# Top-k attention and SwiGLU: scaling by the softmax sum moved behind the product with V, and a pipeline of two turns instead of four

## The chip, the cores and the metric

The kernel runs on one core of a Trainium2 chip. The metric is the device time of one execution in microseconds (us), given as the median over runs. In the profile, PE is the tensor engine (PEld its weight loads), DVE the vector engine, ACT the scalar engine, POOL the GpSimd engine, and SP the engine that issues most DMAs. Every engine works through its own queue strictly in order.

## What is computed

Attention with 8 batches, 8 heads, 576 positions and 64 dimensions per head keeps, for each query, the 32 largest scores; its output, seen as 4608 tokens of 512 numbers, goes through a SwiGLU block with 1536 hidden units. All is float32.

```python
scores = scale * np.matmul(q, k.transpose(0, 1, 3, 2))
kth = np.partition(scores, -top_k, axis=-1)[..., -top_k:-top_k + 1]
scores = np.where(scores >= kth, scores, -1000000000.0)
scores = scores - np.max(scores, axis=-1, keepdims=True)
attn = np.exp(scores)
attn = attn / (np.sum(attn, axis=-1, keepdims=True) + 1e-09)
x = np.matmul(attn, v)              # (B,H,S,D) -> (B*S, H*D)
g = x @ w_gate
out = (g / (1 + np.exp(-g)) * (x @ w_val)) @ w_out
```

## The kernel before

Attention is cut into 160 units: batch, a tile of 128 queries (`qt` 0 to 3) or the last 64 queries (`qt` 4), and a pair of heads. A unit of `qt` 0 to 3 holds two heads as 1152 columns on 128 partitions and is called a two-head unit here. In a unit of `qt` 4 the 64 queries of both heads stack to 128 partitions and 576 columns; the code calls it one head. A batch has 16 two-head and 4 one-head units.

The main loop (from line 729) makes one turn per unit. In turn n, DVE does the top-k of unit n (`select`): four rounds of MAX8 with three rounds of MATCH_REPLACE between, and a last pass (line 339) that writes a penalty mask into `e`. The other steps belong to units before or after n and stand in the same turn, so that each engine's order is written out by hand; at the end of the program the order of PE, DVE, ACT and POOL is pinned. SP's order is left to the scheduler.

In turn n before the change:

- `penalize(n-1)`: POOL computes the bias (line 349) and adds scores and mask (line 351).
- `turn(n-3)`: PE transposes the weights of unit n-3 (line 387), nine 128x128 blocks in a two-head unit; ACT copies them to `et` (line 388).
- `values(n-4)`: PE multiplies by V (lines 407 and 416); ACT copies the result into `xT` (line 431), the FFN's input.
- `scores(n+1)`: PE computes the next unit's scores (lines 308, 294); ACT copies them into `sc` (lines 313, 299).
- `weigh(n-1)`: ACT takes exponentials with their sums (line 360) and adds eps to the sums (line 365).
- `normalize(n-2)`: DVE takes reciprocals (line 372, after the fourth of the seven steps of its top-k), and ACT scales `e` by them (line 375).

Between these steps PE gets pieces of the FFN (`pieces`, `piece`, `feed`). A piece is four matmuls of 256 columns. A block of 256 tokens can start when all four head pairs of its queries are in `xT`. It has 24 product steps of four matmuls of 256 columns (line 471), whose results ACT and POOL combine into `h` (lines 496 to 504), and then seven quarters of six matmuls each (line 557). The quarters are a Strassen-like form of the output product, seven products of half-size blocks instead of eight, and need sums of `h` that POOL makes (lines 564, 572, 577, 605) and sums of results (line 543). The first block uses a plain output product. How many pieces a turn gets is set by `share`: 6.4 less the cost of the attention steps of that turn, in units of a piece. The ACT and POOL parts of a piece are put in lists and emitted at the next `flush`.

In the first 14 turns the weights are brought into a rounded form beside all that (`rounded`, lines 105 to 123: DMA, three ACT operations, one on DVE, two on POOL).

PSUM holds eight banks: five are shared by scores, transposes and products with V, and three by the FFN.

Of the kernel before, what the change touches and what calls it, by code (L numbers as in the profile page):

```python
# [8 lines left out]
AF = mybir.ActivationFunctionType  # L9
ALU = mybir.AluOpType  # L10
FP32 = mybir.dt.float32
# [4 lines left out]
P = 128  # L16
# [3 lines left out]
EPS = 1.0e-9  # L20
# [5 lines left out]
def kernel(  # L26
# [37 lines left out]
    nc = tc.nc  # L64
    B, H, S, D = q.shape
    DM, DFF = w_gate.shape
    J = S // P
    JP = J * P
    R = S - JP
# [9 lines left out]
    consts = ctx.enter_context(tc.tile_pool(name="consts", bufs=1))  # L79
    ld = ctx.enter_context(tc.tile_pool(name="ld", bufs=2))  # L80
    slabs = ctx.enter_context(tc.tile_pool(name="slabs", bufs=4))
    work = ctx.enter_context(tc.tile_pool(name="work", bufs=2))
# [2 lines left out]
    ffn = ctx.enter_context(tc.tile_pool(name="ffn", bufs=2))  # L85
    ps_t = ctx.enter_context(tc.tile_pool(name="ps_t", bufs=5, space=PSUM))
    ps_f = ctx.enter_context(tc.tile_pool(name="ps_f", bufs=3, space=PSUM))

    ident = consts.tile([P, P], FP32, name="ident")
    make_identity(nc, ident[:])  # L90
# [2 lines left out]
    for i in range(NV):  # L93
        vt = consts.tile([P, P], FP32, name=f"vlast{i}")
        nc.vector.memset(vt[:], 0.0)
        vlast.append(vt)
    eps = consts.tile([P, 1], FP32, name="eps")
    nc.vector.memset(eps[:], EPS)
    wg = consts.tile([P, KC, DFF], FP32, name="wg")
    wv = consts.tile([P, KC, DFF], FP32, name="wv")  # L100
    wo = consts.tile([P, MC, DM], FP32, name="wo")
# [170 lines left out]
    state = {}  # L272
# [5 lines left out]
    def scores(n):  # L278
        b, qt, hp = units[n]
        slab = preps[b * NHP + hp]  # L280
        sc = work.tile([P, 2 * S], FP32, tag="sc", name="sc", bufs=2)
        halves = [slice(0, D), slice(D, P)]
        half = S // 2

        def bank():
            return ps_t.tile([P, 512], FP32, tag="t", name="s")


        if qt == J:
            banks = [bank() for _ in range(2)]  # L290
            for i, ps in enumerate(banks):
                for d in halves:
                    k0 = R + i * half
                    nc.tensor.matmul(  # L294
                        ps[d, 0:half], slab[d, S + R : S + 2 * R], slab[d, k0 : k0 + half]
                    )
            yield
            for i, ps in enumerate(banks):
                nc.scalar.copy(sc[:, i * half : (i + 1) * half], ps[:, 0:half])  # L299
        else:  # L300
            q0 = S + 2 * R + qt * P
            banks = []
            for i in range(2):
                for hh, d in enumerate(halves):
                    ps = bank()
                    banks.append((i + 2 * hh, ps))
                    k0 = (1 - hh) * R + i * half
                    nc.tensor.matmul(  # L308
                        ps[:, 0:half], slab[d, q0 : q0 + P], slab[d, k0 : k0 + half]
                    )  # L310
            yield
            for i, ps in banks:
                nc.scalar.copy(sc[:, i * half : (i + 1) * half], ps[:, 0:half])  # L313
        state[n] = dict(sc=sc)

    def select(n):

        nh = n_heads(units[n][1])
        sc = state[n]["sc"]
        m = small.tile([P, 2, TOP_K], FP32, tag="m", name="m", bufs=2)  # L320
        heads = [slice(t * S, (t + 1) * S) for t in range(nh)]
        rest = work.tile([P, 2 * S], FP32, tag="rest", name="rest", bufs=1)
        e = work.tile([P, 2 * S], FP32, tag="e", name="e", bufs=4)
        state[n] |= dict(m=m, e=e, heads=heads)
        cur = sc
        rounds = TOP_K // 8
        for r in range(rounds):
            for t, hs in enumerate(heads):
                nc.vector.max(m[:, t, 8 * r : 8 * r + 8], cur[:, hs])  # L329
                yield  # L330
            if r < rounds - 1:
                for t, hs in enumerate(heads):
                    nc.vector.match_replace(  # L333
                        rest[:, hs], m[:, t, 8 * r : 8 * r + 8], cur[:, hs], LOWEST
                    )
                    yield
                cur = rest
        for t, hs in enumerate(heads):
            nc.vector.tensor_scalar(  # L339
                e[:, hs], sc[:, hs], m[:, t, TOP_K - 1 : TOP_K], FAR, ALU.is_lt, ALU.mult  # L340
            )
# [12 lines left out]
    def weigh(n):  # L354

        st = state[n]
        e, heads, bias = st["e"], st["heads"], st.pop("bias")
        tot = small.tile([P, 2], FP32, tag="tot", name="tot")
        for t, hs in enumerate(heads):
            nc.scalar.activation(  # L360
                e[:, hs], e[:, hs], AF.Exp, bias=bias[:, t : t + 1], scale=scale,
                accum_out=tot[:, t : t + 1],
            )
        nh = len(heads)
        nc.scalar.activation(tot[:, 0:nh], tot[:, 0:nh], AF.Identity, bias=eps[:])
        st["tot"] = tot

    def normalize(n):
        st = state[n]
        tot, e, heads = st.pop("tot"), st["e"], st.pop("heads")  # L370
        nh = len(heads)
        nc.vector.reciprocal(tot[:, 0:nh], tot[:, 0:nh])  # L372
        yield
        for t, hs in enumerate(heads):
            nc.scalar.mul(e[:, hs], e[:, hs], tot[:, t : t + 1])  # L375

    def turn(n):

# [19 lines left out]
    def values(n):  # L398

        b, qt, hp = units[n]  # L400
        vt, v_last, vl = vs[b * NHP + hp]
        et = state.pop(n)["et"]
        last = qt == J
        ql = R if last else P
        av = ps_t.tile([P, P], FP32, tag="t", name="av")
        if not last:
            nc.tensor.matmul(av[:], vl[:], et[:, J, :], start=True, stop=False)  # L407
        for c in range(J + 1 if last else J):
            kl = R if c == J else P
            for hh in range(2):  # L410
                moving = (
                    et[0:kl, c, hh * R : (hh + 1) * R]
                    if last
                    else et[:, c + hh * (J + 1), :]
                )
                nc.tensor.matmul(  # L416
                    av[hh * R : (hh + 1) * R, 0:ql],
                    v_last[:, hh, :] if c == J else vt[:, hh, c, :],
                    moving,
                    start=last and c == 0,  # L420
                    stop=c == (J if last else J - 1),
                )
        c0 = b * S + qt * P
        at = c0
        while at < c0 + ql:
            kb = at // BLK
            n_c = min((kb + 1) * BLK, c0 + ql) - at
            if kb not in xT:
                xT[kb] = ffn.tile([P, NHP, BLK], FP32, tag="xT", name="xT", bufs=3)
                done[kb] = 0  # L430
            nc.scalar.copy(
                xT[kb][:, hp, at - kb * BLK : at - kb * BLK + n_c],
                av[:, at - c0 : at - c0 + n_c],
            )
            done[kb] += n_c
            at += n_c
# [270 lines left out]
    def run(steps):  # L707
        for _ in steps:
            pass
# [13 lines left out]
    run(fetch(1))  # L723
    credit = [0.0]
    no = iter(())
    over = {}
    TURN, VALUES = 3, 4
    due = [2.0]
    for n in range(NU + VALUES):
        nh = n_heads(units[n][1]) if n < NU else 1  # L730
        topk = select(n) if n < NU else no
        over[n - 1] = normalize(n - 1) if 0 <= n - 1 < NU else no
        nxt = scores(n + 1) if n + 1 < NU else no
        ahead = fetch(n + 2) if n + 2 < NU else no
        norm = over.pop(n - 2, no)

        def dve(k, beside=True):

            for _ in range(k * nh):
                next(topk, None)  # L740
                due[0] += 5 / 6 if beside else 0
                if due[0] >= 1:
                    due[0] -= 1
                    rounding(1)

        if n >= NU - NHP:
            credit[0] = 8.0
        else:
            credit[0] = min(credit[0] + share(n), share(n) + 1)
        flush(on_act)  # L750
        if 0 <= n - 1 < NU:
            penalize(n - 1)
        flush(on_pool)
        if 0 <= n - TURN < NU:
            run(turn(n - TURN))
        if n >= VALUES:
            finish_unit(n - VALUES)
        next(nxt, None)

        early[0]()  # L760
        if 0 <= n - 1 < NU:
            weigh(n - 1)
        run(nxt)


        dve(2, beside=False)
        if 2 <= n + 2 < NHP:
            load(n + 2)
        if n < NHP:
            load_v(n)  # L770
        pieces(2)
        flush(on_act)
        dve(1)
        dve(1)
        next(norm, None)
        run(norm)

        flush(on_pool)
        next(ahead, None)
        pieces(1)  # L780
        next(ahead, None)
        dve(1)
        pieces(1)
        dve(2, beside=False)
        run(topk)
        pieces(6)
# [50 lines left out]
```

## Time and profile before

| | |
|---|---|
| median of 3 runs | 1821.17 us (1820.94 to 1823.55) |
| span of the profiled execution | 1817.8 us; the runs' median lies 3.4 us above it |
| instructions | 30526 |
| PE, DVE, ACT, POOL busy | 1708.7, 1610.7, 1218.7, 1036.4 us |
| DMA moved | 59.65 MB, mean 33 GB/s |

The profiled execution's own time is not recorded apart from its span, so that the two are compared through the median. Busy time is the union of an engine's instructions. Lines of the timeline give the start in us from the span's start, the duration, engine, source line, operation, what is written and read, and a count; idle time before the instruction and what ended it stand in brackets. An fp32 matmul appears in the profile as two records.

### The profile page before, as it was taken

The page shows a single profiled execution, that of the slowest core. Times are in us where ns is not written, and L with a number is a line of the kernel's source. Part 1 is how long each engine was busy: PE and PEld are TensorE (multiplying, and loading weights), DVE is VectorE, ACT ScalarE, POOL GpSimd, SP SyncE. Part 2 cuts the span into 40 slices and gives each one's busy share as a digit, 9 for nine tenths or more (in the row PEclk, how much of TensorE's full clock was granted, in tenths as well). Part 3 has the DMA queues.
Part 4 walks back from the last instruction along what each step waited for, and adds up shares of the span by engine and source line. Part 5 has one row for each costly group of instructions (what it writes and reads, how often), then busy time and mean ns, then how long its engine had stood idle before and what let it go on. Part 6 is the DMA issues. An engine that isn't in the chain of part 4 may idle for free.

```text
span 1817.8 us, 30526 instructions
## 1 busy us (share of the span) xinstructions
PE 1708.7 (94%) x10756; PEld 1409.2 (78%) x10756; DVE 1610.7 (89%) x3372; ACT 1218.7 (67%) x2977; POOL 1036.4 (57%) x930
## 2 busy tenths in 40 slices
PE   4458999899999899999999999999999999999999
PEld 2346778687788788887888878887888878888887
DVE  7999999999999799997999989998999989998400
ACT  6778666676667676666767676767676766675532
POOL 5788756455565645554455636564556554646354
PEclk6669999899999999999999999999999999999999
DMA  7432030002100030000300021000300011000000
GB/s 191 125 108 90 14 85 7 12 1 50 45 1 13 2 82 12 13 1 22 73 12 2 13 56 39 1 12 3 74 19 13 1 36 33 1 13 12 1 12 12
DMA packets 109305, 59.65 MB, mean 33 GB/s; under 512 B 88544, under 2 KB 96992, under 8 KB 109152
## 3 DMA queue, kind: packets, MB, share of 16 engines
q1 hardware_dynamic: 108016, 57.37, 12.1%
q8 instruction: 85, 1.39, 0.3%
q14 instruction: 68, 0.56, 0.1%
q10 hardware_dynamic: 1136, 0.33, 0.1%
HBM read 48.23 MB, written 9.44 MB: 32 GB/s over the span
## 4 chain that ended last, share of the span: by engine, by line
PE 86%; DVE 8%; ACT 2%; POOL 2%; issue 2%; DMA 0%; SPq 0%; ACTq 0%; POOLq 0%
PE f L471 41%; PE x_ps L557 9%; PE av L416 8%; PE etps L387 7%; PE s L308 7%; PE y_ps L557 7%; DVE m L329 3%; DVE rest L333 3%; PE s L294 2%; PE av L407 1%; PE o_ps L517 1%; PE kqps L263 1%; DVE size L121 1%; DVE e L339 0%; POOL p L543 0%
## 5 line engine op out<-in xcount | busy, mean ns | idle before, releaser
L329 DVE MAX8 m<-rest 128x8 f32<-128x576 f32 x864 | 612.7, 744 | 2.2
L351 POOL TENSOR_TENSOR e<-e,sc 128x1152 f32<-128x1152 f32 (+1 forms) x160 | 383.1, 2394 | 83.7 <-DVE e L339 76.3
L333 DVE MATCH_REPLACE8 rest<-m,rest 128x576 f32<-128x576 f32 x576 | 423.1, 740 | 0.0
L471 PE MATMUL f<-xT,wg 128*128 128x256 f32 x1728 | 401.6, 382 | 0.0
L471 PE MATMUL f<-xT,wv 128*128 128x256 f32 x1728 | 399.1, 382 | 0.0
L471 PEld LDWEIGHTS f<-xT,wg 128*128 128x128 f32 x1728 | 323.1, 190 | 62.6 <-issue 21.3
L471 PEld LDWEIGHTS f<-xT,wv 128*128 128x128 f32 x1728 | 324.5, 190 | 58.7 <-issue 16.6
L499 POOL TENSOR_TENSOR h<-h,half_g 128x512 f32<-128x512 f32 x108 | 138.2, 1280 | 292.7 <-ACT h L498 292.2
L329 DVE MAX8 m<-sc 128x8 f32<-128x576 f32 x288 | 205.0, 747 | 104.0 <-ACT sc L299 57.8
L388 ACT COPY et<-etps 128x512 f32<-128x512 f32 (+1 forms) x448 | 184.1, 483 | 131.0 <-PE etps L387 130.2
L360 ACT ACTIVATE e<-e,bias 128x576 f32<-128x576 f32 x288 | 222.1, 777 | 57.5 <-POOL e L351 57.2
L387 PE MATMUL etps<-ident,e 128*128 128x128 f32 (+1 forms) x1312 | 184.5, 286 | 79.3 <-POOL size L122 18.2
L504 POOL TENSOR_TENSOR h<-h,val 128x512 f32<-128x512 f32 x108 | 139.6, 1293 | 186.3 <-ACT val L503 186.1
L387 PEld LDWEIGHTS etps<-ident,e 128*128 128x128 f32 (+1 forms) x1312 | 159.6, 147 | 106.0 <-POOL size L122 20.7
L375 ACT ACTIVATE e<-e,tot 128x576 f32<-128x576 f32 x288 | 212.0, 790 | 0.9 <-DVE tot L372 0.9
L333 DVE MATCH_REPLACE8 rest<-m,sc 128x576 f32<-128x576 f32 x288 | 211.5, 740 | 0.0
L308 PE MATMUL s<-kqT 64*128 64x288 f32 x1024 | 178.8, 449 | 14.1 <-ACT kqT L268 8.3
L339 DVE TENSOR_SCALAR e<-sc,m 128x576 f32<-128x576 f32 x288 | 177.2, 651 | 3.4
L416 PE MATMUL av<-et,v 128*64 128x128 f32 (+1 forms) x2560 | 170.3, 278 | 0.0
L313 ACT COPY sc<-s 128x288 f32<-128x288 f32 x512 | 164.0, 402 | 2.9 <-PE s L308 2.9
L496 ACT ACTIVATE h<-f 128x512 f32<-128x512 f32 x108 | 65.2, 604 | 133.3 <-PE f L471 133.3
L416 PEld LDWEIGHTS av<-et,v 128*64 128x64 f32 x2560 | 134.1, 143 | 22.8 <-issue 6.8
(73 smaller groups left out, 2029.1 us busy)
## 6 DMA issues: line engine op xcount, KB each, us to landing
v<-in_v_dram SPq DMA_DIRECT2D x32, 256.0 KB, 2.9
kq_in<-in_k_dram SPq DMA_DIRECT2D x63, 128.0 KB, 2.8
kq_in<-in_q_dram SPq DMA_DIRECT2D x63, 128.0 KB, 3.0
w<-in_moe_w_gate_dram SPq DMA_DIRECT2D x12, 512.0 KB, 3.7
w<-in_moe_w_val_dram SPq DMA_DIRECT2D x12, 512.0 KB, 3.8
w<-in_moe_w_out_dram SPq DMA_DIRECT2D x12, 512.0 KB, 3.5
out_dram<-o SPq DMA_DIRECT2D x38, 128.0 KB, 2.4
out_dram<-o SPq DMA_DIRECT2D x16, 256.0 KB, 2.4
```

Source lines behind the costliest of these rows:

```text
L308: nc.tensor.matmul(ps[:, 0:half], slab[d, q0 : q0 + P], slab[d, k0 : k0 + half])
L329: nc.vector.max(m[:, t, 8 * r : 8 * r + 8], cur[:, hs])
L333: nc.vector.match_replace(rest[:, hs], m[:, t, 8 * r : 8 * r + 8], cur[:, hs], LOWEST)
L339: nc.vector.tensor_scalar(e[:, hs], sc[:, hs], m[:, t, TOP_K - 1 : TOP_K], FAR, ALU.is_lt, ALU.mult)
L351: nc.gpsimd.tensor_tensor(e[:, every], e[:, every], sc[:, every], ALU.add)
L360: nc.scalar.activation(e[:, hs], e[:, hs], AF.Exp, bias=bias[:, t : t + 1], scale=scale, accum_out=tot[:, t : t + 1],)
L375: nc.scalar.mul(e[:, hs], e[:, hs], tot[:, t : t + 1])
L387: nc.tensor.transpose(ps[0:kl, c * P : (c + 1) * P], e[:, k0 : k0 + kl], ident[:])
L388: nc.scalar.copy(et[0:kl, c0 : c0 + cn, :], ps[0:kl, 0 : cn * P].rearrange("p (c j) -> p c j", c=cn),)
L416: nc.tensor.matmul(av[hh * R : (hh + 1) * R, 0:ql], v_last[:, hh, :] if c == J else vt[:, hh, c, :], moving, start=last and c == 0, stop=c ...
L471: nc.tensor.matmul(ps[:, i, :], w[:, kc, m * P : (m + 1) * P], x[:, kc, :], start=(kc == 0), stop=(kc == KC - 1),)
L557: nc.tensor.matmul(ps, lhsT, T[i][m], start=m == 0, stop=m == MQ - 1)
```

## The change

The scaling by the reciprocal of the softmax sum is taken off the weights and put behind the product with V. `normalize` goes. The new `invert(n)` adds eps and takes the reciprocal on DVE, writes the reciprocals of a unit to a small DRAM tile and reads them back broadcast over partitions into `inv`, since the product with V has queries along its columns. `values` now copies its result to `avs`, and the new `scale_up(n)` multiplies `avs` by `inv` into `xT` on POOL.

The distance between steps falls: `turn` runs for unit n-1 and `values` for n-2 (`TURN`, `VALUES` are 1 and 2 instead of 3 and 4). `turn` moves from the start of a turn to its middle, behind two FFN pieces and the third step of DVE's top-k; `invert(n-1)` follows one step later, and then `scale_up(n-2)`. Buffers: `sc` three instead of two, `e` two instead of four.

```diff
+    dram = ctx.enter_context(tc.tile_pool(name="dram", bufs=4, space=bass.MemoryType.DRAM))
...
-    eps = consts.tile([P, 1], FP32, name="eps")
-    nc.vector.memset(eps[:], EPS)
...
-        sc = work.tile([P, 2 * S], FP32, tag="sc", name="sc", bufs=2)
+        sc = work.tile([P, 2 * S], FP32, tag="sc", name="sc", bufs=3)
...
-        e = work.tile([P, 2 * S], FP32, tag="e", name="e", bufs=4)
+        e = work.tile([P, 2 * S], FP32, tag="e", name="e", bufs=2)
...
-        nc.scalar.activation(tot[:, 0:nh], tot[:, 0:nh], AF.Identity, bias=eps[:])
...
-    def normalize(n):
...
+    def invert(n):
+        st = state[n]
+        tot, heads = st.pop("tot"), st.pop("heads")
+        nh = len(heads)
+        nc.vector.tensor_scalar_add(tot[:, 0:nh], tot[:, 0:nh], EPS)
         nc.vector.reciprocal(tot[:, 0:nh], tot[:, 0:nh])
-        yield
-        for t, hs in enumerate(heads):
-            nc.scalar.mul(e[:, hs], e[:, hs], tot[:, t : t + 1])
+        row = dram.tile([2, P], FP32, tag="row", name="row")
+        inv = small.tile([P, P], FP32, tag="inv", name="inv", bufs=3)
+        if nh == 1:
+            nc.sync.dma_start(row[:, 0:R], tot[:, 0:1])
+        else:
+            nc.sync.dma_start(row[:].rearrange("h q -> q h"), tot[:])
+        ql = R if nh == 1 else P
+        for hh in range(2):
+            nc.sync.dma_start(
+                inv[hh * R : (hh + 1) * R, 0:ql],
+                row[hh : hh + 1, 0:ql].to_broadcast([R, ql]),
+            )
...
+        avs = small.tile([P, P], FP32, tag="avs", name="avs", bufs=2)
+        nc.scalar.copy(avs[:, 0:ql], av[:, 0:ql])
...
+    def scale_up(n):
...
-            nc.scalar.copy(
+            nc.gpsimd.tensor_tensor(
                 xT[kb][:, hp, at - kb * BLK : at - kb * BLK + n_c],
-                av[:, at - c0 : at - c0 + n_c],
+                av[:, here], inv[:, here], ALU.mult,
             )
...
-    TURN, VALUES = 3, 4
+    TURN, VALUES = 1, 2
...
-        if 0 <= n - TURN < NU:
-            run(turn(n - TURN))
         if n >= VALUES:
             finish_unit(n - VALUES)
...
         pieces(2)
         flush(on_act)
         dve(1)
+        if behind:
+            run(turn(n - TURN))
         dve(1)
-        next(norm, None)
-        run(norm)
+        if behind:
+            invert(n - TURN)
+        if n >= VALUES:
+            scale_up(n - VALUES)
```

In the changed kernel's file the lines after the pools are numbered one to twenty higher or lower: the transposes are line 396, the products with V 416 and 425, the copy of their result 433, the add of eps and the reciprocal 370 and 371, the DRAM write and reads 375 to 380, the multiply 451, the FFN product 491, the quarters 577.

More of the change, by code (lines that the diff above doesn't have):

```diff
@@ L363, in weigh @@
             )
+        st["tot"] = tot
+    def invert(n):
+        st = state[n]
+        tot, heads = st.pop("tot"), st.pop("heads")
         nh = len(heads)
-        nc.scalar.activation(tot[:, 0:nh], tot[:, 0:nh], AF.Identity, bias=eps[:])
-        st["tot"] = tot
-    def normalize(n):
[L369 to L372, printed above, removed]
-        yield
-        for t, hs in enumerate(heads):
-            nc.scalar.mul(e[:, hs], e[:, hs], tot[:, t : t + 1])
+        nc.vector.tensor_scalar_add(tot[:, 0:nh], tot[:, 0:nh], EPS)
+        nc.vector.reciprocal(tot[:, 0:nh], tot[:, 0:nh])
+        row = dram.tile([2, P], FP32, tag="row", name="row")
[10 more added lines that the diff above has]
+            )
+        st["inv"] = inv
     def turn(n):
@@ L401, in values @@
         vt, v_last, vl = vs[b * NHP + hp]
-        et = state.pop(n)["et"]
+        et = state[n].pop("et")
         last = qt == J
@@ L422, in values @@
                 )
+        avs = small.tile([P, P], FP32, tag="avs", name="avs", bufs=2)
+        nc.scalar.copy(avs[:, 0:ql], av[:, 0:ql])
+        state[n]["av"] = avs
+    def scale_up(n):
+        b, qt, hp = units[n]
+        st = state.pop(n)
+        av, inv = st["av"], st["inv"]
+        ql = R if qt == J else P
         c0 = b * S + qt * P
@@ L430, in values @@
                 done[kb] = 0
-            nc.scalar.copy(
+            here = slice(at - c0, at - c0 + n_c)
+            nc.gpsimd.tensor_tensor(
                 xT[kb][:, hp, at - kb * BLK : at - kb * BLK + n_c],
-                av[:, at - c0 : at - c0 + n_c],
+                av[:, here], inv[:, here], ALU.mult,
             )
@@ L725 @@
     no = iter(())
-    over = {}
-    TURN, VALUES = 3, 4
+    TURN, VALUES = 1, 2
     due = [2.0]
@@ L731 @@
         topk = select(n) if n < NU else no
-        over[n - 1] = normalize(n - 1) if 0 <= n - 1 < NU else no
         nxt = scores(n + 1) if n + 1 < NU else no
         ahead = fetch(n + 2) if n + 2 < NU else no
-        norm = over.pop(n - 2, no)
+        behind = 0 <= n - TURN < NU
         def dve(k, beside=True):
@@ L750 @@
         flush(on_act)
-        if 0 <= n - 1 < NU:
-            penalize(n - 1)
+        if behind:
+            penalize(n - TURN)
         flush(on_pool)
-        if 0 <= n - TURN < NU:
-            run(turn(n - TURN))
         if n >= VALUES:
@@ L760 @@
         early[0]()
-        if 0 <= n - 1 < NU:
-            weigh(n - 1)
+        if behind:
+            weigh(n - TURN)
         run(nxt)
@@ L773 @@
         dve(1)
+        if behind:
+            run(turn(n - TURN))
         dve(1)
-        next(norm, None)
-        run(norm)
+        if behind:
+            invert(n - TURN)
+        if n >= VALUES:
+            scale_up(n - VALUES)
         flush(on_pool)
```

## The prediction

> **What bounds the kernel now.** I read the page's busy time and slices, then the stage windows, the chain that ended last, the waits, and the timelines of two turns.
>
> ```profile
> PE 1708.7 (94%) x10756; PEld 1409.2 (78%) x10756; DVE 1610.7 (89%) x3372; ACT 1218.7 (67%) x2977; POOL 1036.4 (57%) x930
> PE   4458999899999899999999999999999999999999
> DVE  7999999999999799997999989998999989998400
> PEclk6669999899999999999999999999999999999999
> PE 86%; DVE 8%; ACT 2%; POOL 2%; issue 2%; DMA 0%; SPq 0%; ACTq 0%; POOLq 0%
> ```
>
> In the first four slices (182 us) PE is half idle at a granted clock of 0.6 to 0.7, for no FFN block is complete yet. After that PE is nearly full:
>
> ```profile
> 372.00:1760.00 1388.00, 1370.51 (x8837) 1142.19 (x8832) 1251.26 (x2635) 932.48 (x2310) 766.08 (x707) 1.00 0.09 22
> ```
>
> That row's columns are the window, PE, PEld, DVE, ACT and POOL busy, granted clock, DMA share, GB/s. PE idles 17 us in 1388. DVE is second: from the first MAX8 of turn 20 (238.0) to that of turn 156 (1672.8) lie 112 two-head turns of 11.1 us on average, while DVE's own work in one is 10.56 (below: 953.17 to 963.73). DVE's slack is 0.55 us a turn. One-head turns average 7.9 us, DVE's work in one being 6.25. The result therefore hangs on two things: PE's idle start, and whether PE stays fed.
>
> One turn of before (unit n's top-k on DVE):
>
> ```profile
> 953.17 1.42 DVE L329 MAX8 m<-sc 128x8 f32<-128x576 f32 x2
> 955.32 2.63 POOL L351 TENSOR_TENSOR e<-e,sc 128x1152 f32<-128x1152 f32 x1
> 958.16 1.15 PE L387 MATMUL etps<-ident,e 128*128 128x128 f32 x9
> 958.31 1.28 POOL L499 TENSOR_TENSOR h<-h,half_g 128x512 f32<-128x512 f32 x1 [0.35 <-ACT h L498]
> 958.72 0.16 DVE L372 RECIPROCAL tot<-tot 128x2 f32<-128x2 f32 x1
> 960.76 0.78 ACT L360 ACTIVATE e<-e,bias 128x576 f32<-128x576 f32 x1
> 963.73 1.42 DVE L329 MAX8 m<-sc 128x8 f32<-128x576 f32 x2
> ```
>
> DVE runs 5 us ahead of PE's turn (953.17 against 958.16). The exponentials of unit n-1 end at 962.4, 3.7 us after the reciprocal's slot; nobody minds, for that reciprocal is of unit n-2 and the transposes are of n-3. The distance of four turns is slack.
>
> **The change, part by part.**
>
> *FFN starts earlier.* In the built instruction order the first product stands two turns earlier on PE (behind the 11th group of scores instead of the 13th), and behind the last group of scores 44.25 pieces of FFN are left instead of 52 (a piece is 4 matmuls, 8 records). A run of 40 records takes 8.83 us in the chain, so a piece is 1.77 us, and 7.75 x 1.77 = **-13.7 us**: work that now fills the idle start. It is worth nothing if PE loses as much later.
>
> *Removed ACT work.* Line 375 (288 x 0.79) and line 365 (160 x 0.30) go, the copy of av stays (0.27). ACT has 2% of the chain and its long waits are for PE; the saved 259 us count as 0.
>
> *Two turns instead of four.* Now the transposes of n-1 need the exponentials of the same turn, and DVE's add and reciprocal need them too. Call X their end, D and P the starts of DVE's and PE's turn. X is at least D+4.5 (bias and add 0.24+2.63, two exponentials 1.63) and P+3.5 (values 1.6, copy 0.27, exponentials). PE reaches the transposes at P+6.4 (values 1.6, scores 1.24, two pieces 3.54), or P+5.5 where the pieces are quarters (1.33 each). DVE can't start its next turn before X+5.2 (reciprocal and the rest of a turn, 958.72 to 963.73, and the add). Around the loop, X to next X is 9.7 against a turn of 11.1: an ordinary turn holds, with about 1.4 us of DVE slack and 3 us of PE slack. Before, D could run 5 us ahead; now 2. Turns carry 4 or 5 pieces by turns, 0.9 us either side of the mean: I take 0.1 us per two-head turn, 112 x 0.1 = **+11 us** (bounds 0 and 0.3, so 0 to 34).
>
> *Late exponentials in the quarters.* The second FFN product has POOL work queued ahead of the add of line 351:
>
> ```profile
> 1107.92 1.46 PE L557 MATMUL y_ps<-wo,h 128*128 128x256 f32 x6
> 1111.51 2.11 POOL L605 TENSOR_TENSOR h<-h,xT 128x256 f32<-128x256 f32 x3
> 1113.75 2.63 POOL L351 TENSOR_TENSOR e<-e,sc 128x1152 f32<-128x1152 f32 x1
> 1116.41 0.78 ACT L360 ACTIVATE e<-e,bias 128x576 f32<-128x576 f32 x1 [4.92 <-POOL e L351]
> ```
>
> Quarter 6 ends on PE at 1108.0; copies, sums and line 605 follow on POOL, and X comes at 1118.0, 10 us later. Before, DVE lost 2.2 us to that and PE nothing. Now PE has between quarter 6 and the transposes 0 to 3 pieces (0 to 4 us) and 5.5 us of the next turn: it waits 0.5 to 4.5 us, 2.5 on average, where quarter 6 ends behind its turn's transposes, in some 6 blocks of 10. Over 16 blocks: 16 x 0.6 x 2.5 = **+24 us** (bounds 0, if other work moves so that it always fits, and 72).
>
> *The new DVE add* (line 370, 128x2) is a TENSOR_SCALAR. Its nearest rows:
>
> ```profile
> L339 DVE TENSOR_SCALAR e<-sc,m x288: 490/510/2035, 21.2 to 1722.0; 128x576 f32<-128x576 f32 x144
> L372 DVE RECIPROCAL tot<-tot x160: 143/153/164, 41.5 to 1748.2; 128x2 f32<-128x2 f32 x128, 128x1 f32<-128x1 f32 x32
> ```
>
> (minimum/median/maximum ns.) Line 339 stretches to 2 us when POOL runs at its start, the reciprocal never: of 128 two-head reciprocals 96 began under a running POOL instruction, with 0.68 us left on average over all. So the add costs 0.06 (the eps memset of line 98) to 0.06+0.68. I take 0.3, as the slot now follows the exponentials, when POOL's add is done: DVE's turn becomes 10.56+0.06+0.1 (the reciprocal behind it)+0.3 = 11.0, just under 11.1. In steady state that is covered; 12 starting turns, which DVE bounds, pay 12 x 0.35 = **+4 us** (1 to 10). If POOL's rest is paid in full, DVE's turn is 11.4 and it is the bound (second rival). "SBUF — State Buffer", section "Who interferes with whom", of the Trainium skill says that tensor_scalar may use the port pair shared with GpSimd and then blocks for the whole instruction; line 339's 2035 ns agrees, no row shows it for two elements. By the rule alone the add would pay all 0.68, 128 x 0.68 = 87 us of DVE time; by the reciprocal's row none.
>
> *Reciprocals through DRAM.* Three DMAs a unit on SP, one write and two reads behind it. The rows next to them land in 2.0 us (vlast) to 2.9 (v), issues take 0.37 to 0.62 us: X+0.3 plus 5 to 7 us. The product that needs them (line 451, POOL) follows 9.5 us after X in a two-head turn: hidden. In one-head turns it follows after 7: up to 2 us late, on POOL, ahead of FFN products and of the next add; 28 turns, mostly covered: **+5 us** (0 to 28). No row shows 4-byte pieces into DRAM. "DMA: Bandwidth & Descriptors", section "Specifications", of the Trainium skill calls transfers below 512 B read-modify-write; the trace can't tell what that would add.
>
> *POOL* gets 192 multiplies, at most 0.73 each (the 128x256 row): 7% of its time, off the path except as above.
>
> Sum on the profiled execution: 1817.8 -13.7 +11 +24 +4 +5 = 1848; the runs' median is 3.4 above that span, so **1851 us**. What this kernel's measurement can tell from no change is about 0.2%, 3.6 us.
>
> **The rivals.**
>
> 1. *The slack is enough: faster.* Quarters end early enough, jitter fits the window, the add finds POOL idle: -13.7 +4 = 1811.5 us. For it: 3 us of PE slack in ordinary turns. Against: the 1118.0 above. It decides if PE loses under 0.6 us per block. Chance 0.22.
> 2. *DVE becomes the bound: slower by more.* The add pays all of POOL's rest: 112 x (11.4-11.1) = +34, start 12 x 0.8 = +10, quarters now cost DVE X+5.2 as well, 16 x 2.5 = +40; less 13.7: about 1891 us. For it: line 339's maxima. It decides from 0.4 us per add on. Chance 0.18.
> 3. *SP's queue.* SP is in order; at the batch's end the reads of inv stand behind next-batch loads that wait for PE's preparation of keys. If two of four one-head turns lose 5 us in 7 batches, that is +70 on top of the main sum less its 5: 1916 us. Against: before's SP waits stand where nothing needs SP. Chance 0.08.
> 4. *It cancels:* late starts eat just the gain, 1821 us. Chance 0.06.
>
> The forecast itself has 0.46; its own range is 1832 to 1880 (quarters 12 to 48, jitter 3 to 16).
>
> **How the numbers follow.** 1851 is the likeliest case. The range reaches down to rival 1 with its best start (1808) and up past rival 2 (1905); outside lie rival 3 and its like and a tail of rival 1, together under 0.2. Faster by over 0.2%: rival 1 and a little of the main case's lower end, 0.24; within: 0.06; slower: 0.70.
>
> **What would show it.** First product of FFN some 24 us earlier; PE waits at the transposes (now line 396) for exponentials of 1 to 4 us, once a block, 20 to 50 us in all; DVE waiting for ACT's exponentials at line 370 in many turns; line 370 between 60 ns and 1.5 us; no POOL wait for inv in two-head turns. Wrong, if PE's idle time after 372 us stays near 17 us (then rival 1), or if DVE is 98% busy there and PE is not (rival 2), or if POOL's waits for inv exceed 30 us (rival 3).

## The result, and the profile after

The changed kernel takes 2196.8 us (median of 4 runs, 2185.6 to 2203.6) against 1821.2 us before: a ratio of 1.205 (95% interval 1.202 to 1.209). That is 375 us slower, where 30 us slower was forecast. The profiled execution has a span of 2194.0 us.

The page after, first the busy time and the slices, then the chain that ended last:

```profile
PE 1812.4 (83%) x10756; PEld 1463.8 (67%) x10756; DVE 1637.7 (75%) x3531; ACT 980.5 (45%) x2497; POOL 1105.4 (50%) x1122
...
PE   4337878689779987899779986989778996899969
...
DVE  7666867888669875799669975989668985889520
...
PEclk7558989889889998999899997999989998999979
...
PE 32%; DMA 31%; POOL 12%; DVE 9%; ACT 8%; SPq 4%; issue 4%; POOLq 0%; ACTq 0%; DVEq 0%
```

No engine is the bound any more: PE fell from 94% to 83% of the span and DVE from 89% to 75%. Transfers hold 31% of the chain; before they held 0%. The same window as before (columns: window, PE, PEld, DVE, ACT, POOL busy, clock, DMA share, GB/s):

```profile
372.00:1760.00 1388.00, 1202.21 (x7293) 980.21 (x7292) 1118.23 (x2414) 628.78 (x1638) 685.37 (x713) 0.93 0.13 24
```

PE now idles 186 us in these 1388, where it idled 17. Its granted clock over the whole span is 0.90 instead of 0.97, and the same 10756 records keep it busy 104 us longer; what that adds to the time by itself is not shown. The waits (who waited, for whom: us in total, times, longest), engines first, then SP's queue:

```profile
POOL xT L451 <- DMA inv<-row: 676.9, 106, 16.9
DVE tot L370 <- ACT e L359: 431.1, 101, 15.2
ACT e L359 <- POOL e L350: 422.7, 113, 14.6
PEld etps L396 <- ACT e L359: 340.4, 76, 14.0
PE etps L396 <- ACT e L359: 308.5, 66, 13.6
```

```profile
SPq L380 <- DMA row<-tot: 1229.3, 158, 10.7
```

SP's line is where the chain starts. SP waits 7.8 us on average for each unit's row to reach DRAM before it may issue the reads of `inv`. POOL waits at line 451 for `inv`, with the add (line 350) of the unit after next behind it in its queue. ACT's exponentials wait for that add, and DVE's add and PE's transposes wait for the exponentials. Three turns of the timeline show it:

```profile
1405.25 0.53 SPq L377 DMA_DIRECT2D row<-tot  x1
...
1408.60 0.46 POOL L451 TENSOR_TENSOR xT<-avs,inv 128x128 f32<-128x128 f32 x1 [3.88 <-DMA inv<-row]
...
1414.69 1.09 SPq L380 DMA_DIRECT2D inv<-row  x2
...
1416.80 0.36 SPq L377 DMA_DIRECT2D row<-tot  x1
...
1426.12 0.46 POOL L451 TENSOR_TENSOR xT<-avs,inv 128x128 f32<-128x128 f32 x1 [11.20 <-DMA inv<-row]
...
1426.20 1.08 SPq L380 DMA_DIRECT2D inv<-row  x2
...
1427.95 2.60 POOL L350 TENSOR_TENSOR e<-e,sc 128x1152 f32<-128x1152 f32 x1
...
1430.59 0.78 ACT L359 ACTIVATE e<-e,bias 128x576 f32<-128x576 f32 x1 [7.14 <-POOL e L350]
...
1431.51 0.91 PE L396 MATMUL etps<-ident,e 128*128 128x128 f32 x3 [3.55 <-ACT e L359]
```

The write issued at 1405.25 releases the reads only at 1414.69. The trace also records every packet and every engine's landing. The write's packets of 4 B had all been moved by 1408.12, yet its 16 landings came one after another from 1409.2 to 1414.6: the time goes after the data has left. The reads of 1414.69 suffer too. Their packets of 512 B were moved by 1418.2, but the next row's write was issued 2 us after the first of them, its packets moved on the DMA engines in the same microsecond (1417.4 to 1418.3), and 11 of their 32 landings came only between 1423.8 and 1426.0. POOL started at 1426.12.

Worked out over the whole trace in the same way (from issue to last landing): a two-head row takes 8.4 us (median, after turn 14), a one-head row 9.9 us. Of POOL's 676.9 us of waits for `inv`, 317 fall into the last two turns of a batch and the first two of the next. Other transfers that fall beside such a write are late as well: the 12 loads of `w_gate` land after 9.8 us (median) instead of 3.7, and a store took up to 14.1 us against at most 4.4 before.

### The profile page after: what moved, and what is told of

It is laid out like the page before. It is cut to its first block, busy times and chain, and to the rows that moved or that the text cites. A ratio compares the mean times of both kernels' runs of the same rounds, so it can differ in the third digit from the quotient of the medians.

```text
span 2194.0 us, 31671 instructions
## 1 busy us (share of the span) xinstructions
PE 1812.4 (83%) x10756; PEld 1463.8 (67%) x10756; DVE 1637.7 (75%) x3531; ACT 980.5 (45%) x2497; POOL 1105.4 (50%) x1122
## 4 chain that ended last, share of the span: by engine, by line
PE 32%; DMA 31%; POOL 12%; DVE 9%; ACT 8%; SPq 4%; issue 4%; POOLq 0%; ACTq 0%; DVEq 0%
DMA row<-tot 16%; PE f L491 16%; DMA inv<-row 7%; POOL e L350 5%; DVE m L328 4%; ACT e L359 4%; PE x_ps L577 3%; DVE rest L332 3%; PE etps L396 3%; DMA w<-in_moe_w_gate_dram 3%; PE av L425 3%; PE y_ps L577 2%; DMA w<-in_moe_w_val_dram 2%; PE s L307 2%; DMA kq_in<-in_k_dram 2%
## 5 line engine op out<-in xcount | busy, mean ns | idle before, releaser
L396 PE MATMUL etps<-ident,e 128*128 128x128 f32 (+1 forms) x1312 | 227.0, 317 | 316.3 <-ACT e L359 308.5
L451 POOL TENSOR_TENSOR xT<-avs,inv 128x128 f32<-128x128 f32 (+1 forms) x192 | 75.9, 402 | 761.7 <-DMA inv<-row 676.9
L491 PE MATMUL f<-xT,wg 128*128 128x256 f32 x1728 | 426.1, 397 | 25.8 <-POOL xT L451 25.8
L396 PEld LDWEIGHTS etps<-ident,e 128*128 128x128 f32 (+1 forms) x1312 | 169.9, 157 | 378.8 <-ACT e L359 340.4
L491 PE MATMUL f<-xT,wv 128*128 128x256 f32 x1728 | 413.8, 389 | 0.0
L491 PEld LDWEIGHTS f<-xT,wg 128*128 128x128 f32 x1728 | 335.1, 199 | 93.7 <-POOL xT L451 28.8
L370 DVE TENSOR_SCALAR tot<-tot 128x2 f32<-128x2 f32 (+1 forms) x160 | 35.7, 223 | 431.3 <-ACT e L359 431.1
L307 PE MATMUL s<-kqT 64*128 64x288 f32 x1024 | 167.3, 447 | 9.1 <-ACT kqT L267 9.0
L338 DVE TENSOR_SCALAR e<-sc,m 128x576 f32<-128x576 f32 x288 | 169.2, 624 | 5.3 <-PE kqps L262 0.9
L433 ACT COPY avs<-av 128x128 f32<-128x128 f32 (+1 forms) x160 | 40.7, 255 | 274.4 <-PE av L425 270.6
```

What stands on the lines that cost most here:

```text
L307: nc.tensor.matmul(ps[:, 0:half], slab[d, q0 : q0 + P], slab[d, k0 : k0 + half])
L338: nc.vector.tensor_scalar(e[:, hs], sc[:, hs], m[:, t, TOP_K - 1 : TOP_K], FAR, ALU.is_lt, ALU.mult)
L396: nc.tensor.transpose(ps[0:kl, c * P : (c + 1) * P], e[:, k0 : k0 + kl], ident[:])
L491: nc.tensor.matmul(ps[:, i, :], w[:, kc, m * P : (m + 1) * P], x[:, kc, :], start=(kc == 0), stop=(kc == KC - 1),)
```

## Experiments

Theory W: the write of 4-byte pieces into DRAM lands 8 us after its issue and does all this. Rival P: two turns are too few, whatever the transfers take. Rival Q: three more DMAs in SP's in-order queue are too many, whatever each takes. Times are medians; `before` beside them had 1819.7 to 1822.2 us.

### No transfer at all

```diff
-        row = dram.tile(...)   # and the write and the two reads
-        st["inv"] = inv
+        st["inv"] = inv_all    # a constant tile
```

> Left out: the write and the two reads of each unit; inv is one constant tile, so the outputs are not scaled by the right reciprocals; add and reciprocal on DVE stay. Theory W (the 4-byte write into DRAM lands some 8 us after its issue, SP waits behind it, other transfers are held up with it, and POOL waits at line 451): nothing of that is left, and the prediction's sum without its term for the reciprocals holds, 1817.8 - 13.7 + 11 + 24 + 4 = 1843, plus 3 = 1846 us (1810 to 1880). Rival P (two turns between top-k and V are too few, whatever the transfers do): over 2000 us. Rival Q (three more DMAs in SP's in-order queue, whatever each takes): as theory W here.

1844.1 us, 1.012 (1.011 to 1.014) of before. Rival P falls: the short pipeline with the new add, copies and multiplies costs 23 us. The other 353 us belong to the transfers.

### The row as two pieces of 512 B

```diff
+        src = small.tile([2, P], FP32, tag="src", name="src")
+        nc.vector.memset(src[:], 1.0 / 32)
-            nc.sync.dma_start(row[:].rearrange("h q -> q h"), tot[:])
+        nc.sync.dma_start(row[:, 0:ql], src[:, 0:ql])
```

> One change to the kernel after: the row is written from a stand-in tile of 2 partitions that DVE fills behind the reciprocal, as 2 pieces of 512 B (256 B in a one-head unit) instead of 256 (128) pieces of 4 B; the two reads, their order and all waits stay. Left out: the reciprocals' values. Theory W: the write lands in 2 to 3 us like other transfers, SP waits about 2 us for it instead of 7.8, POOL's waits for inv fall from 677 us to under 100, and the time comes within 40 us of the kernel without any transfer, about 1870 us. Rival Q (the three DMAs in SP's order): over 2100 us. Rival P (two turns are too few): over 2100 us.

1851.5 us, 1.016 (1.015 to 1.018). Three DMAs in the same order, with a quick write, cost 7.5 us over none, so rival Q falls. SP's wait for the write and POOL's for `inv` in this kernel:

```profile
SPq L379 <- DMA row<-src: 116.9, 130, 2.8
```

```profile
POOL xT L450 <- DMA inv<-row: 46.9, 11, 7.2
```

Both shrink to less than a tenth (1229.3 and 676.9 above). What is left for POOL is a matter of SP's order: in 9 of its 11 waits, 38 of the 46.9 us, six loads for the next batch stand between the write of a one-head row and its reads, which go out 2.8 to 4.4 us after the row has landed. Here the row landed at 682.0, and the reads were issued at 686.4:

```profile
680.17 0.40 SPq L377 DMA_DIRECT2D row<-src  x1
681.07 0.60 SPq L224 DMA_DIRECT2D kq_last<-in_k_dram  x1
681.76 2.50 SPq L220 DMA_DIRECT2D kq_in<-in_k_dram  x2
684.31 1.30 SPq L220 DMA_DIRECT2D kq_in<-in_q_dram  x2
685.65 0.63 SPq L224 DMA_DIRECT2D kq_last<-in_q_dram  x1
686.39 1.18 SPq L379 DMA_DIRECT2D inv<-row  x2
```

```profile
689.71 0.32 POOL L450 TENSOR_TENSOR xT<-avs,inv 128x64 f32<-128x64 f32 x1 [5.93 <-DMA inv<-row]
```

### The row in SBUF, and pieces far apart in DRAM

```diff
# row_in_sbuf
-        row = dram.tile([2, P], FP32, tag="row", name="row")
+        row = small.tile([2, 1, P], FP32, tag="row", name="row", bufs=4)
...
+        for t in range(2):       # one DMA for each head, 128 pieces of 4 B
+            nc.sync.dma_start(row[t : t + 1, 0, 0 : P // 2 * nh], ...)
# apart
+        row = rows[n % 4]        # DRAM tiles [P, 2 * P], filled at the start
+        apart = row[:].rearrange("q (h c) -> q h c", h=2)[:, 0:nh, 0]
+        nc.sync.dma_start(apart, tot[:, 0:nh])
```

> One change to the kernel after: the row lies in SBUF, on 2 partitions, instead of DRAM. The same number of 4-byte pieces is written (as two DMAs of 128 pieces, one for each head, so one DMA more on SP in each unit), and the two reads broadcast from there. Theory W1 (a 4-byte write is slow because it goes into DRAM): the writes land within 3.5 us and the time comes near that of two_pieces, 1851 us: 1845 to 1880. Rival W2 (256 pieces are slow wherever they go): SP still waits 7 us or more a unit, over 2050 us.

> One change to the kernel after: the 256 (128) pieces of 4 B go into DRAM 512 B apart from each other instead of side by side in 1 KB; the reads bring 512 B from the same tile, filled at the start, so waits, queue and reads are as before. Left out: the reciprocals' values, except one of each head. Theory W1a (pieces that fall into the same few lines of DRAM wait for each other): the write lands within 4 us, time under 1900 us. Theory W1b (each 4-byte write into DRAM is slow by itself): the landing stays at 7 to 9 us and the time over 2100 us.

1852.6 us (1.018, 1.016 to 1.019) and 1852.2 us (1.018, 1.016 to 1.019). Neither the number of pieces nor their 4 B nor DRAM makes the write slow by itself: 256 pieces of 4 B into DRAM are quick when each starts 512 B behind the one before. Landing of the write in three kernels (minimum, median, maximum), in the order SBUF, apart, and side by side (from idle_bounce below, whose two-head write is the one of the changed kernel):

```profile
DMA to landing us min/median/max: 1.7/2.0/4.7
```

```profile
DMA to landing us min/median/max: 1.4/1.9/4.7
```

```profile
DMA to landing us min/median/max: 6.9/8.1/10.1
```

### How far apart

```diff
+        row = rows[n % 8]
+        s = 2 ** (n % 8)          # distance in elements
+        flat = row[:].rearrange("a b -> (a b)")[0 : nh * P * s]
+        nc.sync.dma_start(flat.rearrange("(h q s) -> q h s", h=nh, s=s)[:, :, 0], tot[:, 0:nh])
```

> The kernel after, with eight DRAM tiles used in turn; in tile i the pieces of 4 B lie 4, 8, 16, 32, 64, 128, 256 or 512 B apart (unit number modulo 8), so that one run shows the landing time of the write at each distance, 16 two-head units each. The reads bring the same bytes from the tile's front; left out: most of the reciprocals' values. Theory W1a: some 8 us at 4 B, about 2 us at 512 B as in the kernel apart, and a fall between them where a line of DRAM holds a single piece; if the pieces of one line simply queue, the landing shrinks as the number of pieces in a line does. Time between 1852 and 2197 us, say 1950, for the slow units are only some of all.

One run, 1867.7 us. From its landing records, for two-head units after turn 14 (14 or 15 at each distance):

| distance of the pieces, B | 4 | 8 | 16 | 32 | 64 | 128 to 512 |
|---|---|---|---|---|---|---|
| issue to last landing, us (median) | 7.85 | 3.49 | 2.35 | 1.67 | 1.55 | 1.54 to 1.55 |

The floor is reached at 64 B. Above the floor of 1.55 us remain 6.3, 1.9, 0.8 and 0.1 us for 16, 8, 4 and 2 pieces in each 64 B: more than in proportion. So W1a holds, with 64 B as the distance from which pieces no longer hold each other up. What in the memory makes them wait for each other is not shown by these runs.

### What the late write hurts besides POOL

```diff
# idle_bounce: the kernel before, behind its reciprocal
+        nc.sync.dma_start(row[:].rearrange("h q -> q h"), tot[:])
+        for hh in range(2):       # inv is read by nobody
+            nc.sync.dma_start(inv[hh * R : (hh + 1) * R, 0:32], row[...].to_broadcast([R, 32]))
# scale_late
+    TURN, VALUES, SCALE = 1, 2, 4
+            scale_up(n - SCALE)
```

> The kernel before, with the row's write and two reads (32 columns each, for room) added behind each reciprocal; nobody uses what they bring. Theory W: the write still holds up transfers that share the queue: in the first 14 turns the weights' loads land after some 10 us instead of 3.7, and those turns take 30 to 60 us more in all; afterwards nothing waits for a transfer within 8 us, and little is added: 1850 to 1890 us. If only POOL's wait for inv matters: 1821 to 1828 us. Rival Q as well: the start is hurt by SP's order, 1850 or more; so this run prices the start, it does not tell W from Q.

> One change to the kernel after: the product that needs inv (line 451) works on unit n-4 instead of n-2, some 20 us later, with more buffers for avs, inv and row; transposes and products with V stay where they are. Theory W: POOL's waits for inv fall from 677 us to under 60; what stays is the hurt start (about 59 us) and the FFN's start two turns later (13.7 us): 1846 + 59 + 14 = 1920 us (1880 to 1960). Rival P (two turns are too few for transposes and V): over 2100 us.

1927.7 us (1.059, 1.056 to 1.062) and 1998.7 us (1.097, 1.095 to 1.099): both above what I expected, because I priced only the start. The waits say what I left out, first for idle_bounce and then for scale_late:

```profile
ACT e L362 <- DMA row<-tot: 97.7, 37, 6.5
```

```profile
PE kqps L262 <- DMA kq_in<-in_k_dram: 65.6, 8, 10.4
...
ACT size L113 <- DMA w<-in_moe_w_gate_dram: 37.4, 6, 9.4
...
POOL xT L451 <- DMA inv<-row: 23.3, 8, 8.5
```

In idle_bounce nobody reads `inv`, but the write still holds its source `tot`, which has three buffers: the exponentials of a later unit wait to overwrite it. In scale_late POOL's wait for `inv` is nearly gone (23.3 us), and what is left is other transfers held up: weights in the start, and the next batch's keys, which PE needs in the second turn of a batch (turns 101, 121 and 141 take 20 to 21 us, against 10.6 to 11.7 before; the loads of keys issued at 1441.2 and 1441.8 landed 8.4 and 10.2 us later).

That splits the cost of the slow write, by differences of times. With a quick write the kernel takes 1852; scale_late starts the FFN two turns later, worth 14 by the prediction's price, so about 1999 - 1852 - 14 = 133 us are late loads, and the other 2197 - 1999 + 14 = 212 us are POOL's wait for `inv`. The 14 is an estimate.

### The small part: what the two-turn pipeline costs

```diff
# no_wait: no_bounce, and
-        if behind:
-            invert(n - TURN)
+        if n >= VALUES:           # at the start of DVE's turn
+            invert(n - VALUES)
```

> The kernel no_bounce (no transfer, wrong scale) with DVE's add and reciprocal one turn later, at the start of DVE's turn for unit n-2, so that DVE never waits there for the exponentials of its own turn. In no_bounce DVE waits 103.6 us in 49 waits at the add, and its turn 20 starts 19 us later than in the kernel before. If those waits cost the start, this gives 1844 - 8 = 1836 us (1828 to 1840), as rows_two's turn 20 began 8 us earlier; if only PE's waits at the transposes count: 1844 again.

1825.0 us (1.002, 1.001 to 1.003): 19 us less than no_bounce, more than twice what I expected. Where DVE's add and reciprocal stand is therefore worth most of the pipeline's net 23 us. The move does not end DVE's waits at the add: 54.6 us in 19 waits are left of 103.6 in 49. It changes the add's own time too, as the add can be held by POOL (see the account of the prediction): the 19 adds before turn 20 take 6.3 us instead of 15.6. The run does not part the two. Of the 17.6 us between the two profiled spans, 6 had been gained by turn 20 of DVE (251.5 against 257.2), 11 by turn 40 and 13 by turn 156.

```diff
# sbuf_early: row_in_sbuf, with invert(n - VALUES) as in no_wait
# sbuf_later: the same, and
         pieces(1)
+        if behind:
+            run(turn(n - TURN))
```

> A complete version of the two-turn pipeline from the two repairs that paid: the row lies in SBUF (row_in_sbuf), and DVE's add and reciprocal of unit n-2 stand at the start of DVE's turn n (no_wait); the product that needs inv follows in the same turn, some 8 us later, and the two transfers take 2 + 3 us. If the two repairs add up: 1852.6 - 19 = 1834 us, at best 1825 as in no_wait; if the later reciprocal makes inv late for POOL again: over 1850.

> sbuf_early with the transposes of unit n-1 one FFN piece later in PE's turn (behind three pieces instead of two). In no_wait PE still waits 75 us at the transposes, 21 us of that within 14 us of a block's quarters and 54 us in the start; a piece (1.77 us) put ahead takes that much off each wait behind the quarters: 16 x 0.6 x 1.8 = 17 us at most, so sbuf_early less 5 to 17 us, 1820 to 1829. If the late copies of the transposes hold up ACT's FFN work instead (as in before_three): 20 us or more above sbuf_early.

1842.8 us (1.012, 1.010 to 1.013) and 1838.0 us (1.009, 1.008 to 1.010). The repairs do not add up: with the reciprocal later, POOL waits 113.4 us for `inv` again (47.6 in row_in_sbuf), and 10 of the 19 us remain. In sbuf_later PE's waits at the transposes within 14 us of a quarter fall from 21.6 to 5.6 us, 16 us as expected, but the time by only 5: ACT's copies of the transposes now wait 215.3 us for PE instead of 88.1.

### Versions meant to beat both

```diff
# rows_two, rows_three: queries as rows of the product with V, scaled by ACT
-                nc.tensor.matmul(av[hh * R : (hh + 1) * R, 0:ql], vt[:, hh, c, :], moving, ...)
+                nc.tensor.matmul(av[:, h], et[:, c + hh * (J + 1), :], vt[:, hh, c, :], ...)
+            nc.scalar.mul(avs[:, h], av[:, h], tot[:, t : t + 1])
+            nc.tensor.transpose(xp[:], avs[:], ident[:])
# before_three: transposes of n-2 late in turn n; before_short: scaling of n-1 late in turn n
-    TURN, VALUES = 3, 4
+    TURN, VALUES = 2, 3           # before_short: 2, 2
```

> A version without any transfer: the product with V is made with queries as rows (the transposed weights are the stationary operand, V moves with 64 columns), ACT scales its rows by the reciprocal while it copies them from PSUM, PE transposes the result (one 128x128 block a unit), ACT copies it into xT. Still two turns between top-k and V; the reciprocal of unit n-2 stands at the start of DVE's turn, where nothing is waited for. The transpose adds 0.13 us of PE a unit (a row of line 396: 9 in 1.15 us); the eight products with V may save between nothing and half of 1.09 us. So 1844 (no_bounce) less DVE's waits for exponentials at the add in the start (up to 13 us), plus 160 x 0.13 = 21 and less 0 to 87: 1760 to 1860 us, likeliest 1810. If products with 64 columns take as long as those with 128: 1850 or more.

> The version rows_two with three turns between top-k and V instead of two (transposes of unit n-2, V of n-3): the transposes no longer need the exponentials of the same turn, the FFN starts one turn earlier than in the kernel before. If the short pipeline's late exponentials cost what the prediction said (24 + 11 us), this is 10 to 30 us below rows_two, 1770 to 1810 us; if those cost nothing, it is about 7 us above rows_two.

> The kernel before, weights scaled on ACT as there, with its pipeline shortened by one turn: the transposes of unit n-2 stand late in turn n, behind the scaling, and the product with V of unit n-3 at the start. FFN starts one turn earlier, half of the prediction's 13.7 us: 1821 - 7 = 1814 us (1808 to 1826); if PE now waits for ACT's scaling in many turns, 1830 or more.

> The kernel before with reciprocal and scaling of unit n-1 late in turn n, the transposes of n-2 at the start and the product with V of n-2 in the middle of the turn: FFN starts about one and a half turns earlier than before (10 us), while every step still has 3 us or more behind the one it needs, except where quarter 6 makes the exponentials late (10 us after it), where DVE's late reciprocal would wait. 1821 - 10 = 1811 us if that does not count, up to 1830 if it costs DVE 1 us per block and jitter as much.

1926.8, 1946.6, 1895.4 and 1884.9 us (1.058, 1.069, 1.041 and 1.036 of before). All four are slower than the likeliest case of their expectations; rows_two and before_three fall into the slow branch that was named, though PE's waits for the scaling, the reason named for before_three, are only 36.1 us there. For the rows versions the reason stands in the groups by shape, first two of rows_two, then one of no_bounce:

```profile
L408 PE MATMUL av<-v,et 128*128 128x64 f32 x2048 | 254.0, 279 | 0.0
L408 PE MATMUL av<-v,et 128*64 128x64 f32 x512 | 21.9, 228 | 6.3 <-ACT et L384 6.3
```

```profile
L415 PE MATMUL av<-et,v 128*64 128x128 f32 x2048 | 148.2, 289 | 0.0
```

With 64 moving columns a record costs PE 254.0 / 2048 = 0.124 us on a 128x128 stationary block and 21.9 / 512 = 0.043 on a 128x64 block; with 128 columns on a 128x64 block it costs 0.072. On these rows half the columns save 0.029 us and twice the block costs 0.081, and PE's busy time rose by 113 us, the 47 us of the new transposes included.

In before_three, ACT waits 231.2 us at the copies of the transposes (130.2 before), and DVE waits 161.2 us for copies of scores, which stand behind them on ACT (103.9 before). In before_short, DVE's late reciprocal waits 168.3 us for ACT's sums. These two causes are read from the waits alone, and why rows_three is 20 us slower than rows_two is open. No version here beats the kernel before.

## Why the prediction was wrong

**The failed step** is *Reciprocals through DRAM*. It put the write at 2.0 to 2.9 us from rows that were all loads of larger pieces into SBUF, counted X + 0.3 plus 5 to 7 us for `inv` (X is the end of the exponentials), and bounded the term at 0 to 28 us. The write takes 8 to 10 us and the reads 3.9 (median), so with the prediction's X + 0.3 `inv` comes at X + 0.3 + 8.4 + 3.9 = X + 12.6, 3 us after its need even in two-head turns; measured from X to the last landing it is 14.6 us there (median, after turn 14). Each delay moves all that follows on POOL. The term was +5. With a write that lands in 1 to 2 us it is 7.5 to 8.5 us (two_pieces, apart, row_in_sbuf, each against no_bounce), so the size was near for a quick write, though not its reason: what POOL waits for there is in the main reads that stand behind the next batch's loads (two_pieces: up to 6.1 us), and not a product that comes 2 us too early in one-head turns. For the real write it is 353 us. I had written that no row shows 4-byte pieces into DRAM, and took the end nearest to the rows I had; the upper bound should have carried the case that all of POOL's and SP's queues stand behind this write.

**The rule I could not weigh** said that transfers below 512 B are read-modify-write ("DMA: Bandwidth & Descriptors", section "Specifications", of the Trainium skill). The runs show that size alone sets no price: pieces of 4 B land in 1.9 us at 512 B distance. It is pieces less than 64 B apart that wait.

**Rival 3** named the right queue, and its sign came: POOL waits 676.9 us for `inv`, over 30. Its mechanism, loads of the next batch ahead of the reads, is not what costs 353 us: in 158 of 160 units SP issues the first read within 0.4 us of the row's last landing. It is most of what two_pieces has left (38 us of POOL's waits). Its price, 1916 us, came from one-head turns alone.

**The rest of the sum** came to 1846 us on the scale of the runs, and no_bounce took 1844. That agreement is luck in part, as two errors of some 15 us each cancel: the start cost 15 us more than its term, and the turns after it 16 less than theirs. The terms one by one:

- FFN earlier, -13.7: from DVE's turn 156 to the end 130.5 us in no_bounce and 145.0 before, so -14.5. The first FFN product came at 135.2 us instead of 150.5, 15 us earlier and not 24; in the changed kernel it came at 178.2.
- Start, +4: too small. Turn 20 starts 257.2 us into the span instead of 238.0, so +19. The 19 adds before it take 15.6 us, 0.82 each, and DVE waits 9.0 us ahead of them for exponentials; the mask pass takes 6.3 us less. The term had 0.35 for each of 12 turns and no wait.
- Quarters and jitter, +24 and +11: from turn 20 to turn 156 no_bounce loses 19 us in all, where I had 35. It is PE's idle time, as forecast: 43.2 us in this stretch instead of 24.8, with the same busy time (no_bounce, then before; columns as above).

```profile
257.20:1711.10 1453.90, 1410.75 (x9102) 1172.55 (x9103) 1382.60 (x3002) 782.94 (x2037) 858.01 (x892) 0.99 0.09 23
```

```profile
238.00:1672.80 1434.80, 1410.00 (x9098) 1170.57 (x9097) 1357.68 (x2866) 983.41 (x2449) 800.84 (x727) 0.99 0.09 23
```

- PE's gaps of over 0.3 us at the transposes within 14 us after a quarter sum to 23.5 us in no_bounce (20 gaps), but before had 12.0 us of them (5 gaps): the quarters cost about half of their 24.
- The add itself: 271 ns on average in no_bounce, which hides two cases. Of 51 adds that began with more than 0.15 us left of a POOL instruction, 41 ended about 0.03 us after that instruction; the other 10, and the 106 that began with POOL idle, took 0.13 to 0.17 us. So the add mostly does pay POOL's rest when it meets one, as the prediction worked out by the rule alone, and in the start it cost what rival 2 said, 0.8 us a turn. After turn 20 it took 0.20 us on average, because it seldom met a POOL instruction there; so rival 2's +34 did not come. One of the long ones:

```profile
81.48 1.27 DVE L372 TENSOR_SCALAR tot<-tot 128x2 f32<-128x2 f32 x1
```

```profile
81.27 1.44 POOL L124 TENSOR_TENSOR wg<-size,w 128x512 f32<-128x512 f32 x1
```

PE's waits at the transposes for exponentials, forecast at 20 to 50 us, are 86.2 us in no_bounce. Of these, 58 lie in the first 260 us, where the gaps ahead of the transposes came to 57 us before as well; the 28.6 us behind the start lie in the forecast.

## What to carry to other kernels

In these runs a small transfer's price went by where its pieces land, not by its bytes: ask how many lie within 64 B of DRAM, and look in the trace for a write of that shape before taking a load's time for it. Where no row shows it, bound it from above by everything queued behind its landing: the reads on the same issuing queue, other loads on the same DMA engines, the source buffer that it holds, and the instruction behind the one that waits. A shorter pipeline frees its two turns once (14.5 us here); the lost slack can cost something in every turn (19 us from turn 20 to 156, and 19 before).

## What the runs showed of the hardware that I had not expected

- 256 pieces of 4 B into 1 KB of DRAM: packets moved 2.9 us after the issue, last landing 8 to 9.4 us after it. At 8, 16, 32 and 64 B distance: 3.5, 2.35, 1.67 and 1.55 us, then flat. The same pieces into SBUF, side by side: 2.0 us.
- Beside a slow write the landings of transfers issued up to 2 us before it are late, too: reads whose packets had been moved by 1418.2 landed as late as 1426.0. Weight loads land in 9.8 us instead of 3.7 while such writes run.
- A DVE add of 128x2 that began with over 0.15 us left of a POOL instruction ended with that one in 41 of 51 cases (it took up to 1.27 us); with POOL idle it took 0.16 us. A reciprocal of that size took 143 to 164 ns before, although 96 of 128 began under a POOL instruction.
- A one-head row of half as many pieces is no quicker (9.9 us); its landings are recorded on 3 DMA engines instead of 16.
